# A preLN linear-attention and SwiGLU block, forward and backward: up gradients written over the g2 w2^T buffer, its products two chunks ahead, two norms in other rows, early transposes copied in two parts

## The chip, the cores and the metric

The kernel runs on one core of one Trainium2 chip. The metric is the device time of one execution in microseconds (us). The median of three runs before the change is 838.91 us (838.71 to 839.56); the profiled execution has a span of 838.5 us, and its times count from the start of that span.

The five engines that the text names: PE (TensorE, matmuls and transposes), ACT (ScalarE), DVE (VectorE), POOL (GpSimd) and SyncE (SP in the profile, which here only issues DMAs). Each works through its own row of instructions in the order in which the kernel was written. An instruction that waits holds up everything behind it on its engine.

## The reference

One transformer block in bf16, with 2048 tokens, width 640, 32 heads of 20 and an MLP of width 1728. The output of the block and the gradients of its six inputs are returned.

```python
def _A_ref(x, wqkv, wo):            # linear attention
    q, k, v = split(x @ wqkv)
    phi = lambda t: where(t > 0, t + 1, exp(t)) + 1e-6
    pq, pk = phi(q), phi(k)
    kv = einsum("bhsd,bhse->bhde", pk, v)
    z = einsum("bhsd->bhd", pk)
    o = einsum("bhqd,bhde->bhqe", pq, kv) / (einsum("bhqd,bhd->bhq", pq, z) + 1e-6)
    return o @ wo

def _B_ref(x, w1, w3, w2):          # SwiGLU
    return (silu(x @ w1) * (x @ w3)) @ w2

h = x + _A_ref(layernorm(x), wqkv, wo)
h2 = h + _B_ref(layernorm(h), w1, w3, w2)
out, vjp = jax.vjp(block, x, wqkv, wo, w1, w3, w2)
return out, *vjp(grad_out)
```

In the MLP the backward pass needs, for every token and every one of the 1728 channels f, the product g2 w2^T (g2 is `grad_out`); from it and from gate, up and sigmoid come the gradients of gate and of up.

## The kernel before

The tokens are cut into 16 tiles of 128 rows, and four tiles make a group c = 0 to 3 of 512. The width of 640 is five chunks of 128; the MLP's width is 14 f chunks of 128. The order of the work is written out by hand: the lines of the function are the order on every engine, and buffers (tiles of a pool with a number of `bufs`) come round in turn. A new tile of a name waits until everything that reads or writes the tile that had its buffer is done, DMAs included.

**The front (0 to about 60 us).** For each tile: statistics on DVE (`bn_stats` on each half of the row, `bn_aggr`, variance plus epsilon; lines 144 to 152), the rstd by a power on POOL, the norm on DVE in place (line 155), a transpose into `pqT`, and the k and q products on PE (line 255). Tiles 0 to 7 are transposed on PE into PSUM and copied by ACT (`p1_tr`, line 251); tiles 8 to 15 by DMA. The main loop over tiles (line 460) interleaves tile t's products with the transposes, statistics and norms of later tiles. The loads of x stand in SyncE's row: tiles 0, 1, 2, 3 alone, then 4 and 5, 6 and 7, 8 to 11, 12 to 15 (lines 188 to 424), between transposing loads of w2 and of the first group of `grad_out` (`w2T`, `g2T`).

**The second layer norm.** `f2_at(t)` (line 561) makes the attention output of tile t: ten matmuls with `pqT`, which at that point holds the transposed, scaled q rows of tile t, then the add of x. For tiles 5 to 7 and for the second half of tiles 0 to 3, PE adds x and ACT copies the sum; for the others, DVE adds. Statistics follow. `f2_hn(t)` (line 643) norms the tile into `hn`, which has two buffers of its own, and stores it to HBM for the backward pass; `f2_ht(t)` transposes it (tiles 0 to 3 on PE, later ones by DMA) into `hnT`. Tiles 0 to 3 go through this in the long `run(...)` list (line 777), which mixes in late q tiles, eight early g2 w2^T products (`mlp_ghh`), and loads of `w2T`. Rows named `h2`, of the size of `hn`, have two buffers in the same pool; `r_prod` uses them before this point and the MLP's output rows after it.

**The q rows of later tiles.** For tiles 6 to 15, `r_den(t)` makes the denominators on DVE, and `r_end(t)` scales the rows (line 350) and has SyncE transpose them into `pqT` (line 354, which writes what `f2_at(t)` reads). Their places in the MLP are given by `r_steps` (line 818): in group c = 1, `r_end` of tile 11 comes at the end of f chunk 9.

**The MLP (about 105 to 355 us).** For every group c and f chunk: five matmuls of 512 columns for g2 w2^T (`ghh_chunk`, line 364, copied by ACT into a `ghh` buffer), five for gate, five for up. ACT writes sigmoid(gate), sigmoid(-gate) (`s2`), gate and up; the copies of two chunks make a pair. `ghh` has four buffers of a pair each, `sig`, `s2`, `gate` and `up` two each. The seven DVE products of a pair are put in a list and taken from it during the next pair's chunks (`drain`):

```python
        op(gate, gate, sig)
        op(hh, gate, up, to=hh_d)
        op(s2, gate, s2)
        op(gate, gate, gh, to=gg_d, r0=F)
        op(s2, s2, sig, ALU.add)
        op(s2, s2, up)
        op(up, s2, gh, to=gg_d, q=dmaG)
```

The last one writes the up gradients into `up`, and POOL stores them from there to `gg_d`. Eight chunks of g2 w2^T are made before the MLP starts (`FILL = 8`); in the MLP, chunk n makes product n + `AHEAD`, with `AHEAD = 4`, from chunk 4 of c = 0 on. Between the chunks of group c stand the attention, norm and transpose of the tiles of group c + 1; the function `sides` (line 792) gives the chunk of each. For c = 1, tile 11's `f2_at` comes at the end of chunk 11. From c = 1 on, the output products of the group before (`o2_steps`) are mixed in as well. After the MLP come the gradients of w2, of the second norm, of the attention and of w1 and w3.

Of the kernel before, what the change touches and what calls it, by code (L numbers as in the profile page):

```python
# [9 lines left out]
P = 128  # L10
BF16 = mybir.dt.bfloat16
# [7 lines left out]
S, D, H, F = 2048, 640, 32, 1728  # L19
DH = D // H  # L20
ST, DT = S // P, D // P
FT, FP = 14, 1792
FL = F - 13 * P
W, SC, TPC = 512, 4, 4
# [31 lines left out]
def kernel(  # L56
# [20 lines left out]
    dma, dmaT, dmaG = SY.dma_start, SY.dma_start_transpose, G.dma_start  # L77
# [23 lines left out]
    gg_d = dram.tile([2 * F, S], BF16, name="gg_d")  # L101
    r_v, pk_v, xn_v, hn_v, m_v, pq_v = rows(r_d), rows(pk_d), rows(xn_d), rows(hn_d), rows(m_d), rows(pq_d)

    def pool(name, side="left", space=None):
        kw = dict(space=space) if space is not None else dict(side=side)
        return tc.alloc_tile_pool(name=name, bufs=1, reuse_waits="tile", **kw)
# [6 lines left out]
    x_sb = x_ext[:, :, 0:D]  # L113
# [53 lines left out]
    ln1, ln2 = Stats("ln1"), Stats("ln2")  # L167


    pf = pool("pf", "right")  # L170
# [8 lines left out]
    def load_x(a, b):  # L179
        dma(out=x_sb[:, a:b, :], in_=xS[:, a:b, :])  # L180
# [4 lines left out]
    load_wq(3, 4)  # L185
    load_x(2, 3)
    load_x(3, 4)
    load_x(4, 6)

    mask = cp.tile([P, DT, M_MAX, DH], BF16, name="mask")  # L190

# [24 lines left out]
    def load_g2T(c):  # L216
        g2T[c] = U2.tile([P, DT, W], BF16, name="g2T", tag="g2T", bufs=2)
        dmaT(out=g2T[c][:], in_=goD[c * W:(c + 1) * W, :])
# [16 lines left out]
    def on_act(t):  # L235
        return t > XT_DMA and t % 2 == 0

    def p1_norm(t):
        xn = x_sb[:, t, :]
        (ln1.norm_act if on_act(t) else ln1.norm)(xn, xn, t)  # L240
        if t >= XT_DMA:
            dmaT(out=pqT[:, :, t * P:(t + 1) * P], in_=xn)

    def p1_tr(t, parts=((0, DT),)):
        xn = x_sb[:, t, :]
        for a, b in parts:
            tr = ps.tile([P, DT, P], BF16, name="tr", bufs=2)
            for c in range(a, b):
                T.transpose(tr[:, c, :], xn[:, c * P:(c + 1) * P], ident[:])

            A.copy(out=pqT[:, a:b, t * P:(t + 1) * P], in_=tr[:, a:b, :])  # L251
# [6 lines left out]
    def p1_mm(t, n0):  # L258
        acc = ps.tile([P, 2, 512], F32, name="big", bufs=2)
        for j in range(2):  # L260
            p1_half(acc[:, j, 0:HD], t, n0 + j * HD)
        return acc
# [6 lines left out]
    def phi(acc, dst, then=None):  # L269

        mq, rq = (p1.tile([P, D], BF16, name=n, bufs=b) for n, b in (("mq", 3), ("rq", 3)))
        A.activation(two(mq[:]), acc[:, :, 0:HD], AF.Exp)
        A.activation(two(rq[:]), acc[:, :, 0:HD], AF.Relu)

        def rest():
            V.tensor_scalar(out=mq[:], in0=mq[:], scalar1=1.0, scalar2=1e-6, op0=ALU.min, op1=ALU.add)
            V.tensor_tensor(out=dst, in0=mq[:], in1=rq[:], op=ALU.add)
            if then is not None:
                then()
        held.append(rest)  # L280

    def phi_rest(keep=0):
        while len(held) > keep:
            held.pop(0)()
# [14 lines left out]
    def q_tile(t):  # L299
        q_home(t)  # L300
        phi(p1_mm(t, 0), pqs[t])
# [66 lines left out]
    def ghh_chunk(n, acc):  # L368

        c, fc = divmod(n, FT)  # L370
        mm5_to(acc, w2T, fc, g2T[c])
        if n % 2 == 0:
            ghh[n // 2] = pf.tile([P, 2, W], BF16, name="ghh", bufs=4)
        A.copy(out=ghh[n // 2][:, n % 2, :], in_=acc[:])  # L374
# [5 lines left out]
    def m_part(m, tiles):  # L380
        if m not in macc:
            macc[m] = [ps.tile([P, 512], F32, name="macc", tag=("m", "tr")[m % 2], bufs=2) for _ in range(2)]
        for t in tiles:
            for j, n in enumerate((HD, HD + (m < 3))):
                T.matmul(macc[m][j][:, 0:n], lhsT=pk_all[:, t, m * P:(m + 1) * P],  # L385
                         rhs=x_ext[:, t, j * HD:j * HD + n], start=(t == 0), stop=(t == ST - 1))
# [25 lines left out]
    def load_w2T(a, b):  # L412
        dmaT(out=w2T[:, :, a:b], in_=B_w2[a:b, :])
# [2 lines left out]

    zero_pads()
    load_w2T(0, 2 * P)
    load_x(6, 8)
    load_g2T(0)  # L420
    load_w2T(2 * P, 4 * P)
    load_x(8, 12)
# [8 lines left out]
        ln1.norm(x_sb[:, 0, a:b], x_sb[:, 0, a:b], 0)  # L431
    p1_tr(0, ((0, 2), (2, DT)))
    for t in (1, 2):
        ln1.part(x_sb, t, 1)
        ln1.part(x_sb, t + 1, 0)
        p1_norm(t)
    ln1.part(x_sb, 3, 1)
    trickle += [lambda: load_wq(4, 6)]
    for c0, c1 in ((0, 2), (2, 4), (4, 5)):
# [13 lines left out]
    def group_out(g):  # L453
        sl = slice(g * TPC, (g + 1) * TPC)
        dma(out=pk_v[:, sl, :], in_=pk_all[:, sl, :])
        if g < 2:
            xn_out(g, dma)

    QT = (5, 7, 9, 11)
    for t in range(ST):  # L460
        g, i = divmod(t, TPC)
        k = p1_mm(t, D)
        if t < 3:
            p1_tr(t + 1)
        for n in stat_of.get(t, ()):
            ln1.run(x_sb, n, n + 1)
            if on_act(n):
                ln1.bias(n)
        for n in norm_of.get(t, ()):
            if not on_act(n):  # L470
                p1_norm(n)
        phi_rest(t < 6)
        phi(k, pk_all[:, t, :])
        if 2 <= t < XT_DMA - 2:
            p1_tr(t + 2)
        for n in norm_of.get(t, ()):
            if on_act(n):
                p1_norm(n)
        if t in QT:
            q_tile(QT.index(t))  # L480
        if 2 <= t < 6:
            ghh_chunk(t - 2, ps.tile([P, 2, 512], F32, name="gp", tag="big", bufs=2)[:, 0])
        if t >= 3:
            m_part(0, [t - 3])
        if t >= 11:
            V.memset(bd[:, t - 11, :], 0.0)
            make_mask(t - 11)
        if t >= 9:
            m_part(1, [2 * (t - 9), 2 * (t - 9) + 1])
        if i == 1 and g > 0:  # L490
            group_out(g - 1)
        elif t >= 2 and trickle:
            trickle.pop(0)()
# [65 lines left out]
    hn, hnT, hhT = {}, {}, {}  # L559
# [81 lines left out]
        dma(out=pqs[t], in_=pq_v[:, t, :])  # L641

    def f2_hn(t):
        hn[t] = pf.tile([P, D], BF16, name="hn", bufs=2)
        ln2.norm(hn[t][:], x_sb[:, t, :], t)
        dma(out=hn_v[:, t, :], in_=hn[t][:])

# [22 lines left out]
    def mlp_ghh(n):  # L670
        if n < SC * FT:
            ghh_chunk(n, ps.tile([P, W], F32, name="mm", bufs=4))

    AHEAD = 4

    def mlp(c, fc, between):

        k, i = divmod(fc, 2)
        n = c * FT + fc
        if n >= FILL - AHEAD:  # L680
            mlp_ghh(n + AHEAD)
        gp = mm5(w1, fc, hnT[c])
# [33 lines left out]
    def mlp_pair(c, k, sig, s2, gate, up, gh):  # L716

        hh = hhT[c][:, 2 * k:2 * k + 2, :]

        def op(out, a, b, alu=ALU.mult, to=None, r0=0, q=dma):  # L720
            def go():
                V.tensor_tensor(out=out, in0=a, in1=b, op=alu)
                if to is not None:
                    store(to, r0, c, k, out, q)
            later.append(go)

        sig, s2, gate, up, gh = (x[:] for x in (sig, s2, gate, up, gh))
# [3 lines that stand above are left out]
        op(gate, gate, gh, to=gg_d, r0=F)  # L731
        op(s2, s2, sig, ALU.add)
        op(s2, s2, up)
        op(up, s2, gh, to=gg_d, q=dmaG)

    def o2_steps(c, q=dma, tag="o2"):

# [33 lines left out]
    def run(*steps):  # L771
# [5 lines left out]
    run((q_late, 10, f2_mT), (f2_kv, 2), (f2_kv, 3), (f2_kv, 4), (phi_rest,), (q_late, 11), (f2_wT, 0), (f2_wT, 1),  # L777
        (phi_rest,), (q_late, 12), (f2_wT, 2), (f2_wT, 3), (phi_rest,), (q_late, 13, lambda: f2_wT(4)),
        (r_red, 3), (r_inv, 3), (r_scale, 3), (r_prod, 5), (load_x, 2, 4), (r_T, 3), (q_late, 14), (r_red, 4),
        (r_inv, 4), (r_scale, 4), (r_T, 4), (load_x, 4, 8), (mlp_ghh, 4), (load_w2T, 8 * P, 10 * P), (q_late, 15),  # L780
        (sig_table,), (f2_half, 0, 0), (f2_half, 1, 0), (f2_half, 0, 1), (f2_half, 1, 1), (f2_hn, 0), (mlp_ghh, 5),
        (f2_half, 2, 0), (f2_hn, 1), (f2_m_out,), (load_w2T, 10 * P, 12 * P), (f2_half, 2, 1),
        (f2_ht, 0), (mlp_ghh, 6), (f2_half, 3, 0), (f2_hn, 2), (f2_w_out,), (f2_ht, 1), (f2_half, 3, 1), (phi_rest, 2),
        (q_out, 10, 14), (f2_ht, 2), (f2_hn, 3), (mlp_ghh, 7), (load_w2T, 12 * P, F), (f2_half, 4, 0), (f2_ht, 3),
        (f2_half, 4, 1), (r4_out,), (r_red, 5), (r_inv, 5), (r_scale, 5), (r_out, 5), (r4b_out,), (q_out, 8, 10))
    p1.release()
    pa = pool("pa", "right")
# [4 lines left out]
    def sides(c):  # L792
        side = ({}, {})
        for i in range(TPC):
            k0 = 3 * i - (i == TPC - 1) + (-2, 1, 0)[c]
            for k, pos, f in ((k0 + 2, 1, f2_at), (k0 + 3, 0, f2_hn), (k0 + 3, 1, f2_ht)):
                if c == 0 and f is f2_at:
                    if i == 0:
                        continue
                    f = f2_at0  # L800
                if k0 == -2 and f in (f2_at0, f2_hn, f2_ht):
                    k, pos = (k + 1, 0) if f is f2_at0 else (k + 1, pos)
                if k >= 0:
                    side[pos].setdefault(k, []).append((f, i))
        return side
# [19 lines left out]
    for c in range(SC):  # L825
# [8 lines left out]
        for fc in range(FT):  # L834
# [22 lines left out]
            if c == SC - 1 and fc in (1, 2, 5, 6):  # L857
                i = (1, 2, 5, 6).index(fc)
# [73 lines left out]
    for fc in range(FT - 1):  # L932
        b, i = divmod(fc, 4)
# [347 lines left out]
    for t in range(ST):  # L1281
        c, i = divmod(t, TPC)
# [136 lines left out]
```

## Time and profile before

| | busy us | share of the span |
|---|---|---|
| PE | 820.6 | 98% |
| DVE | 453.7 | 54% |
| ACT | 317.8 | 38% |
| POOL | 103.8 | 12% |

| stretch of the span | PE busy | DVE busy | ACT busy |
|---|---|---|---|
| 0 to 60 us (front) | 53.58 | 43.40 | 39.13 |
| 80 to 100 us (end of the attention) | 19.55 | 16.84 | 16.67 |
| 100 to 160 us (start of the MLP) | 56.29 | 49.19 | 39.94 |
| 160 to 240 us | 77.89 | 72.62 | 45.83 |
| 240 to 340 us | 100.00 | 72.78 | 60.67 |

The busy times are unions of the instructions' spans. Matmuls overlap, and their ends are modelled, so PE's busy time is a little more than the time in which it makes progress. The granted clock of PE is 1.00 in all slices but the last.

Three views are used below. The list of waits tells which engine sat idle at which line, and which instruction or DMA ended the idle time; its numbers are the total, the count and the longest, in us. The timeline lists instructions in order of time, with start and duration; in brackets stands the idle time before it and what ended it. The DMA view tells how long a DMA took from its issue to its landing.

### The profile page before, as it was taken

Reading aid. Unit: us, or ns where it says so; the run is one execution under the profiler, and the core shown is the slowest. Engines: PE = TensorE matmul, PEld = TensorE weight load, DVE = VectorE, ACT = ScalarE, POOL = GpSimd, SP = SyncE. Lnnn points to the kernel's source line nnn. Section 1 sums busy time; section 2 is a strip of 40 time slices with the busy share of each in tenths; the row PEclk is TensorE's granted clock in tenths of the full one; section 3 lists DMA queues with packets and bytes.
Section 4 is the critical chain, followed back from the end, with each engine's and each line's share of the span. In section 5 each row is a group of like instructions: output and inputs, shape, how many; then the busy total and the mean of one; then the engine's idle time right before and its main releaser. Section 6 shows DMA issues by size and latency. Waiting matters only on the chain.

```text
span 838.5 us, 14175 instructions
## 1 busy us (share of the span) xinstructions
PE 820.6 (98%) x5552; PEld 522.9 (62%) x5552; DVE 453.7 (54%) x964; ACT 317.8 (38%) x603; POOL 103.8 (12%) x152
## 2 busy tenths in 40 slices
PE   7999899999999999999999999999999999999998
PEld 5677544455455555677777777777777777555554
DVE  7947798799988666500037777772681545200000
ACT  5855666755555666111122121222211333311111
POOL 2314222112121101000001111110110000000000
PEclk9999999999999999999999999999999999999999
DMA  9996997778575356899967889436998799875661
GB/s 253 295 275 135 215 248 226 238 198 203 132 202 156 110 164 216 212 237 227 277 162 181 186 194 200 98 82 131 204 242 174 155 197 178 213 188 146 163 166 37
DMA packets 324131, 157.59 MB, mean 188 GB/s; under 512 B 235360, under 2 KB 319232, under 8 KB 324064
## 3 DMA queue, kind: packets, MB, share of 16 engines
q1 hardware_dynamic: 294832, 129.04, 65.8%
q10 hardware_dynamic: 24416, 11.23, 6.5%
q0 software_dynamic: 4816, 16.42, 5.8%
q8 instruction: 43, 0.70, 0.4%
q14 instruction: 24, 0.20, 0.1%
HBM read 48.15 MB, written 51.46 MB: 119 GB/s over the span
## 4 chain that ended last, share of the span: by engine, by line
PE 77%; DMA 9%; DVE 8%; issue 2%; SPq 1%; ACT 1%; POOL 0%; DVEq 0%; ACTq 0%; POOLq 0%
PE job L1184 18%; PE mm L364 14%; PE ghn L986 13%; PE gxn L1343 8%; PE gw L939 7%; PE o L746 5%; PE gwo L1071 3%; PE gr L1043 2%; DMA gg_d<-up 2%; PE macc L385 2%; DVE st L147 2%; PE big L255 2%; DMA pqT<-x_sb 2%; PE at L569 1%; DMA small<-m_d 1%
## 5 line engine op out<-in xcount | busy, mean ns | idle before, releaser
L1184 PE MATMUL job<-gb,hnN 128*128 128x432 bf16 x640 | 117.0, 346 | 0.0
L986 PEld LDWEIGHTS <-ggb 128*128 128x128 bf16 x864 | 84.5, 98 | 32.8
L1184 PEld LDWEIGHTS <-hnN 128*128 128x128 bf16 x640 | 62.6, 98 | 54.1
L364 PE MATMUL mm<-pqT,w 128*128 128x512 bf16 x405 | 93.9, 379 | 1.5 <-DMA pqT<-hn 1.1
L364 PEld LDWEIGHTS <-w 128*128 128x128 bf16 x540 | 52.7, 98 | 65.2 <-DMA pqT<-hn 1.6
L1188 ACT CAST obs<-job 128x432 bf16<-128x432 f32 (+1 forms) x60 | 29.1, 485 | 123.8 <-PE job L1184 123.8
L746 PE MATMUL o<-w,hhT 128*128 128x320 bf16 x448 | 67.7, 299 | 0.2 <-DVE h L751 0.2
L364 PE MATMUL mm<-g2T,w2T 128*128 128x512 bf16 x260 | 64.6, 379 | 2.3 <-ACT up L694 2.3
L986 PE MATMUL ghn<-w13a,ggb 128*128 128x320 bf16 x448 | 63.5, 299 | 0.0
L986 PE MATMUL ghn<-w13b,ggb 128*128 128x320 bf16 x416 | 61.4, 299 | 0.0
L746 PEld LDWEIGHTS <-hhT 128*128 128x128 bf16 x448 | 43.8, 98 | 23.9 <-issue 0.4
L939 PE MATMUL gw<-g,hb 128*128 128x320 bf16 x416 | 57.0, 299 | 0.0
L939 PEld LDWEIGHTS <-hb 128*128 128x128 bf16 x416 | 40.6, 98 | 15.7
L374 ACT CAST ghh<-mm 128x512 bf16<-128x512 f32 x52 | 30.7, 590 | 48.5 <-PE mm L364 45.2
L1343 PE MATMUL gxn<-wqT,gT 128*128 128x320 bf16 x320 | 48.7, 299 | 0.0
L1051 POOL TENSOR_TENSOR sz<-Zb,g_h 128x640 f32<-128x640 bf16 x16 | 20.2, 1261 | 200.2 <-DVE g_h L1049 200.2
L364 PEld LDWEIGHTS <-w2T 128*128 128x128 bf16 x280 | 27.2, 98 | 28.1 <-issue 3.3
L255 PE MATMUL big<-wqkv,pqT 128*128 128x320 bf16 x260 | 39.2, 299 | 4.5 <-ACT pqT L251 1.6
L686 ACT ACTIVATE sig<-mm 128x512 bf16<-128x512 f32 x56 | 33.8, 604 | 25.3 <-PE mm L364 22.8
L255 PEld LDWEIGHTS <-pqT 128*128 128x128 bf16 x320 | 30.5, 98 | 18.1 <-DMA pqT<-x_sb 2.3
L998 ACT ACTIVATE gs<-ghn 128x640 bf16<-128x640 f32 x16 | 11.2, 703 | 78.8 <-PE ghn L986 73.9
L1343 PEld LDWEIGHTS <-gT 128*128 128x128 bf16 x320 | 31.2, 98 | 12.4 <-DMA gT<-g_q 0.3
(195 smaller groups left out, 1246.4 us busy)
## 6 DMA issues: line engine op xcount, KB each, us to landing
hh_d<-hhT SPq DMA_DIRECT2D x24, 256.0 KB, 2.6
gg_d<-gate SPq DMA_DIRECT2D x24, 256.0 KB, 3.6
gg_d<-up POOLq DMA_DIRECT2D x24, 256.0 KB, 2.9
ggb<-gg_d SPq DMA_DIRECT2D x6, 896.0 KB, 5.7
ggb<-gg_d SPq DMA_DIRECT2D x6, 832.0 KB, 6.9
out_dram<-obs ACTq DMA_DIRECT2D x40, 108.0 KB, 2.6
ggb<-gg_d SPq DMA_DIRECT2D x2, 1728.0 KB, 12.8
x_sb<-in_A_x_dram SPq DMA_DIRECT2D x5, 640.0 KB, 6.8
```

What stands on the lines that cost most here:

```text
L255: T.matmul(acc, lhsT=pqT[:, c, t * P:(t + 1) * P], rhs=wqkv[:, c, n0:n0 + HD], start=(c == 0), stop=(c == DT - 1))
L364: T.matmul(acc[:], lhsT=w[:, c, fc * P:(fc + 1) * P], rhs=rhs[:, c, :], start=(c == 0), stop=(c == DT - 1))
L374: A.copy(out=ghh[n // 2][:, n % 2, :], in_=acc[:])
L686: A.activation(sig[:, i, :], gp[:], AF.Sigmoid)
L746: T.matmul(o2["ps"][:, 0:HD], lhsT=hhT[c][:, fc, i * P:(i + 1) * P], rhs=w2[:, fc, j * HD:(j + 1) * HD], start=(fc == 0), stop=(fc == FT - 1))
L939: T.matmul(acc[:, j, 0:HD], lhsT=hb[b][:, t, i * P:(i + 1) * P], rhs=g2[:, t, j * HD:(j + 1) * HD], start=(t == 0), stop=(t == ST - 1))
L986: T.matmul(acc[:, j, 0:HD], lhsT=ggb[t // 2][:, k, lo:lo + P], rhs=rhs[:, j * HD:(j + 1) * HD], start=(k == 0), stop=(k == NG - 1))
L1051: G.tensor_tensor(out=heads(sz[t][:]), in0=heads(Zb[:]), in1=per_head(g_hx[:, t, D:]), op=ALU.mult)
L1071: T.matmul(acc[m][:, j, 0:n], lhsT=r_sb[:, t, m * P:(m + 1) * P], rhs=g_hx[:, t, j * HD:j * HD + n], start=(t == 0), stop=(t == ST - 1))
L1184: T.matmul(acc[:, 0:n], lhsT=lhs[:, t, m * P:(m + 1) * P], rhs=rhs(t), start=(t == 0), stop=(t == ST - 1))
L1188: A.copy(out=ob, in_=acc[:, 0:n])
L1343: T.matmul(acc[:, j, 0:HD], lhsT=g, rhs=wqT[:, k, j * HD:(j + 1) * HD], start=(k == 0), stop=(k == 14))
```

## The change

It has six parts, all of them about buffers and order; the arithmetic stays what it was.

- The last DVE product of a pair writes the up gradients over the `ghh` pair rather than over `up`, and the store reads them from there. `up` is then free after its last product, and a `ghh` buffer is held until its store has landed. To allow for that, the g2 w2^T products run two chunks ahead, not four.
- The later part of `w2T` is loaded in two transfers (2 and 3.5 chunks) in place of three, and later.
- `hn` of tiles 2 and 3 is put in the `h2` buffers, so that these norms need not wait for the stores of tiles 0 and 1.
- In the front, DVE norms tile 1 before it takes up the statistics of tile 2, and x tiles 4 to 7 come in one load.
- The PE transposes of tiles 1 to 3 are copied by ACT in two parts (chunks 0 and 1, then 2 to 4), as tile 0's already were, so that the products can start on the first part.
- In `sides`, `f2_at`, `f2_hn` and `f2_ht` of tile 11 come one f chunk earlier in c = 1.

```diff
-    load_x(4, 6)
+    load_x(4, 8)
...
-    load_x(6, 8)
...
     for t in (1, 2):
-        ln1.part(x_sb, t, 1)
-        ln1.part(x_sb, t + 1, 0)
-        p1_norm(t)
+        if t == 1:
+            ln1.part(x_sb, t, 1)
+            p1_norm(t)
+            ln1.run(x_sb, t + 1, t + 2)
+        else:
+            ln1.part(x_sb, t + 1, 0)
+            p1_norm(t)
...
         if t < 3:
-            p1_tr(t + 1)
+            p1_tr(t + 1, ((0, 2), (2, DT)))
...
     def f2_hn(t):
-        hn[t] = pf.tile([P, D], BF16, name="hn", bufs=2)
+        hn[t] = (pf.tile([P, D], BF16, name="hn", tag="h2", bufs=2) if 2 <= t < TPC else
+                 pf.tile([P, D], BF16, name="hn", bufs=2))
...
-    AHEAD = 4
+    AHEAD = 2
...
-        op(up, s2, gh, to=gg_d, q=dmaG)
+        op(gh, s2, gh, to=gg_d, q=dmaG)
...
-        (r_inv, 4), (r_scale, 4), (r_T, 4), (load_x, 4, 8), (mlp_ghh, 4), (load_w2T, 8 * P, 10 * P), (q_late, 15),
+        (r_inv, 4), (r_scale, 4), (r_T, 4), (load_x, 4, 8), (mlp_ghh, 4), (q_late, 15),
...
-        (f2_half, 2, 0), (f2_hn, 1), (f2_m_out,), (load_w2T, 10 * P, 12 * P), (f2_half, 2, 1),
+        (f2_half, 2, 0), (f2_hn, 1), (f2_m_out,), (load_w2T, 8 * P, 10 * P), (f2_half, 2, 1),
...
-        (q_out, 10, 14), (f2_ht, 2), (f2_hn, 3), (mlp_ghh, 7), (load_w2T, 12 * P, F), (f2_half, 4, 0), (f2_ht, 3),
+        (q_out, 10, 14), (f2_ht, 2), (f2_hn, 3), (mlp_ghh, 7), (load_w2T, 10 * P, F), (f2_half, 4, 0), (f2_ht, 3),
...
-            k0 = 3 * i - (i == TPC - 1) + (-2, 1, 0)[c]
+            k0 = 3 * i - (i == TPC - 1) * (1 + (c == 1)) + (-2, 1, 0)[c]
```

## The prediction

> **What bounds the kernel now.** I read the engine totals first, then the waits of TensorE (PE), then the timeline around each wait.
>
> ```profile
> PE 820.6 (98%) x5552; PEld 522.9 (62%) x5552; DVE 453.7 (54%) x964; ACT 317.8 (38%) x603; POOL 103.8 (12%) x152
> ```
>
> PE is busy for 98% of 838.5 us and its clock is full, so no edit of this diff (which leaves PE's matmul count alone) can gain more than the 17.9 us in which PE stands still. Which of it the diff touches is told by PE's own waits (us in total, times, longest):
>
> ```profile
> PE trh L658 <- DVE hn L155: 2.5, 1, 2.5
> PE mm L364 <- ACT up L694: 2.3, 4, 1.0
> PE big L255 <- ACT pqT L251: 1.6, 2, 0.8
> PE mm L364 <- DMA pqT<-hn: 1.1, 1, 1.1
> PE big L255 <- DMA pqT<-x_sb: 1.0, 2, 0.8
> PE tr L249 <- DVE x_sb L155: 0.7, 2, 0.4
> ```
>
> These six rows, 9.2 us, are the targets. Behind the second row, in the waits of 110 to 165 us, and behind the first, in the timeline of VectorE (DVE):
>
> ```profile
> ACT up L694 <- DMA gg_d<-up: 12.7, 6, 3.7
> ```
> ```profile
> 101.55 0.45 DVE L155 TENSOR_SCALAR hn<-x_sb,ln_mv,ln_rs 128x640 bf16<-128x640 bf16 x1 [2.04 <-DMA hn_d<-hn]
> ```
>
> ScalarE (ACT) waits six times for a store to have landed before it may refill an `up` buffer; DVE waits once for a store of `hn` rows. From 240 us to 820 PE is busy 19.5 to 20 of each 20 us, and all that the diff does there is to put two products back (below).
>
> **What the Trainium skill says.** "Perfetto Trace Analysis", Optimization Strategy: a gap that repeats on the engine that should be saturated can mean too few buffers for the next tile. That is the `up` row: two buffers, each held until a store lands. "DMA: Bandwidth & Descriptors", Anatomy of one DMA: a completion carries about 2 us that do not scale with bytes, because the semaphore waits for the last byte's receipt. The trace agrees and is worse under load: `gg_d<-up` takes a median 2.9 us and up to 7.0. So taking a landing out of a short buffer loop is worth more than shrinking the store. "Perfetto Trace Analysis", Optimizing Scalar/DVE Operations: an unsaturated engine that causes bubbles elsewhere may be split into smaller instructions. The trace has both forms: one 640-wide transposed copy is 0.69 us, the two-part one of tile 0 0.82.
>
> **The front (tiles 0 to 7).** DVE does tile 1's norm only after half of tile 2's statistics, and so sat idle 1.91 us until 8.50, when tile 2 had landed (8.48). With the norm ahead, it starts when POOL's `ln_rs` is out, 6.67 + 0.55 = 7.22, inside that idle time; 0.35 us leaves DVE's unbroken row from 8.5 on. PE's transposes of tile 1 (9.40, ready now at 8.96) gain 0.4, and copies in two parts let matmuls start 0.75 us after the transposes (tile 0: 5.52 to 6.27) instead of 1.24 (9.40 to 10.64), three times: 0.4 + 3 x 0.45 = 1.8 us for PE up to tile 3. But DVE runs without a gap from 9.25 to 41.6 and tile 4's transposes already waited for it (0.29 at 15.34), so only its 0.35 survives. Then PE waits at 41.41 for `pqT<-x_sb`, one of a chain of DMAs that land one behind the other from 32 to 58 us. Merging tiles 4 to 7 into one load saves SyncE one issue of 0.57 before the g2 transpose; that and the earlier norms move this chain by something between 0 and 0.6. The merged load lands about 9.76 + 328 KB at 300 GB/s = 10.9, before DVE needs tile 4 at 11.7. I take **-0.3**, ends 0 and -0.9. The extra ACT copies (3 x 0.13) lie in ACT's idle time there (0.70 before each copy).
>
> **`hn` of tiles 2 and 3 in the h2 rows.** hn(2) then no longer waits for the store of hn(0), issued at 97.46 and landed at 101.45. Its rstd was ready at 98.57; DVE reaches it after its statistics at 99.47, so hn(2) moves from 101.55 to 99.47 and the PE transpose from 102.05 to 99.97. The h2 buffers were last read at 90.5 (`rden` reduction). hn(3), 1.9 us behind in the row, is ready at about 101.9, and PE reaches its transpose at 102.0. The whole stage moves by **-2.1**; ends -1.5 and -2.5. The later and larger `w2T` load costs nothing: SyncE has room, and with products two chunks ahead chunk 8 is used two chunks later.
>
> **`up` over the `ghh` buffer, products two ahead (c = 0).** From chunk 4 (115.58) to c = 1 chunk 2 (162.16) PE took 46.6 us. Its content, at 0.216 us a 512-wide matmul: 35 groups of five, 37.8, plus two `at` pairs at 1.63 and 15 output matmuls 2.0: 43.1. So 3.5 us are stalls (the rows show 2.6, since modelled ends overlap). Without the `up` wait two other limits remain. (a) A `ghh` buffer (four) is now held until its store lands, but the fourth pair later wants it two chunks later than `up` was wanted: pair 0's store landed at 122.27, wanted at 121.6, ACT waits 0.7; pair 2's 138.8, wanted 137.4; both inside ACT's idle time. (b) `s2` (`s` in the trace) has two buffers and is free only after its pair's last DVE product: pair 1's at 126.3, while chunk 6 would be there at 122. ACT sits until 126.3, and PE, with four accumulators, stalls about 0.4 at chunk 7. After that, DVE saves its own 2.9 us wait at 139.98 (it waited for ACT, which waited for `up`) and keeps ahead: pair 3's last product 139.4, wanted 139.2; pair 4's 144.7, wanted 145.1. So 3.5 - 0.4 = **-3.1**, ends -1.0 (if DVE's row binds throughout) and -3.5. Two products (2 x 1.08 us PE) leave c = 0 and return in c = 3, where PE is the bound too: zero in sum.
>
> **`at` of tile 11 one chunk earlier (c = 1).** It is meant to end the 1.1 us wait for `pqT<-hn` at 220.92 (in matmul rate 219.61 to 220.92, 1.3). But `at` of tile 11 reads the scaled q rows of tile 11, and what makes them stays where it was:
>
> ```profile
> 202.68 0.82 DVE L350 TENSOR_TENSOR pql<-pql,rden 128x640 bf16<-128x640 bf16 x1
> 203.60 1.21 SPq L354 DMA_TRANSPOSE pqT<-pql  x1
> ```
> ```profile
> pqT<-pql SPq DMA_TRANSPOSE x1, 4.2
> ```
> ```profile
> 198.92 1.52 PE L569 MATMUL at<-Wp,pqT 128*128 128x320 bf16 x10
> 204.47 1.24 PE L364 MATMUL mm<-g2T,w2T 128*128 128x512 bf16 x5
> 208.79 1.52 PE L569 MATMUL at<-Wp,pqT 128*128 128x320 bf16 x10
> ```
>
> The scale on DVE stands after the adds and statistics of tile 10, and these wait for PE's `at` of tile 10 at 198.92. The transpose lands at 203.60 + 4.15 = 207.75. Before, PE came at 208.79, 1.0 us later. Now it comes at 204.47: a **new wait** of 3.3 us, and since the release is counted from PE's own `at` of tile 10, gains further up do not shorten it. Behind it in PE's row stand all later products; DVE's row also stops for it, at tile 11's add, but it has its own slack of 1 us at 208 and 228. hn(11) then lands at about 218, PE needs it at 222.9. Net +3.3 - 1.3 = **+2.0**; ends +2.3, and -1.3 if the transpose came in time. Transposes of this kind took 3.5 to 4.2 us in this stage, so 0.7 is the play.
>
> **Sum.** -0.3 - 2.1 - 3.1 + 2.0 = -3.5: 838.9 becomes **835.4**.
>
> **Rivals.** (1) No new wait: the transpose of tile 11 is there, because DVE runs ahead of PE once c = 0 is freed. Against it: DVE cannot pass the adds of tile 10. -0.3 - 2.1 - 3.1 - 1.3 gives 832.1; chance 0.12. (2) The wait changes its name in c = 0: DVE's row (no idle from 110.35 to 130) holds `s2` and PE gains only 1.0. For it: 46 us of DVE work (110.35 to 162.4 less 5.6 idle) in that stage; against it: DVE's 2.9 + 1.2 + 1.3 us of idle time there are themselves effects of `up`. 838.9 - 0.3 - 2.1 - 1.0 + 2.0 = 837.5; chance 0.15. (3) Slower: the merged load of tiles 4 to 7 lands behind the transposes (12.7, as the load of 6 and 7 did at 11.8) and puts +1.0 on DVE's row, hn brings 1.0, c = 0 nothing, tile 11 costs 2.0: 840.9. Against it: the load is issued ahead of them. Chance 0.06. My forecast has 0.67.
>
> **The numbers.** The range runs from just under rival 1 to just over rival 2, 832.0 to 837.6; some of rival 1, rival 3 and the worst ends stay out. Faster by 0.2% means below 837.2: the forecast less 0.03, rival 1, and nearly half of rival 2: 0.82. Within: 0.12. Slower: 0.06.
>
> **What would show it.** In the profile after: no row ACT `up` on `gg_d`, a small one ACT `ghh` on `gg_d` or on DVE; `trh` on DVE at most 0.5; a new PE row `at` on DMA `pqT<-pql` of about 3 us near 200 us, and none on `pqT<-hn`. Without that new row, near 832; with new rows of `ghh` or `s` that PE waits for, near 837.5; with tile 4's statistics waiting for `x_sb`, the front is wrong.

## The result and the profile after

The changed kernel takes 837.27 us (median of four executions, 835.47 to 837.44) against 838.88 before: a ratio of 0.9974 with a 95% interval of 0.9957 to 0.9992. The medians are 1.6 us apart, the ratio stands for 2.2. Run again beside the experiments, it took 835.94 us (13 executions) against 836.74 (25): 0.9993, interval 0.9981 to 1.0004, which no longer excludes that nothing is gained. It is a small gain, well below the 3.5 us that the prediction summed up. One execution of all those below, of the kernel with the norms alone, took 1448.05 us and is left out of its ratio. The profiled executions had spans of 838.5 and 835.6 us, 2.9 apart, so the first pair of traces flatters the change by about 1.3 us. For this reason a second pair stands beside it below. Its two traces were taken among the experiments, on two chips on which the median of the kernel before is 836.28 us (before) and 836.74 us (changed).

The engine totals of the changed kernel, the line that answers to the one shown of before:

```profile
PE 820.2 (98%) x5552; PEld 522.5 (63%) x5552; DVE 454.3 (54%) x964; ACT 319.5 (38%) x606; POOL 104.4 (13%) x152
```

PE's work is the same; ACT has three copies more, those of the front. PE's own waits in the changed kernel (us in total, times, longest):

```profile
PE at L572 <- DMA pqT<-pql: 4.4, 3, 2.5
PE big L255 <- ACT rq L273: 1.3, 1, 1.3
...
PE tr L249 <- DVE x_sb L155: 1.1, 1, 1.1
...
PE big L255 <- ACT pqT L251: 0.6, 2, 0.3
...
PE trh L662 <- DVE hn L155: 0.4, 1, 0.4
PE big L255 <- DMA pqT<-x_sb: 0.4, 1, 0.4
```

`trh` on DVE has fallen from 2.5 to 0.4, and the rows of `mm` on ACT `up` (2.3) and on `pqT<-hn` (1.1) are gone. In their place the list is headed by a row that was not there: `at` waits three times for the transposed q rows. PE's timeline shows where (start, duration, instruction; in brackets the idle time before it and what ended it):

```profile
98.85 0.45 PE L662 MATMUL trh<-ident,hn 128*128 128x128 bf16 x5 [0.37 <-DVE hn L155]
...
112.84 0.85 PE L572 MATMUL at<-Wp,pqT 128*128 128x320 bf16 x5 [1.57 <-DMA pqT<-pql]
...
130.64 0.85 PE L572 MATMUL at<-Wp,pqT 128*128 128x320 bf16 x5 [0.34 <-DMA pqT<-pql]
...
197.13 1.11 PE L750 MATMUL o<-w,hhT 128*128 128x320 bf16 x7
200.77 1.53 PE L572 MATMUL at<-Wp,pqT 128*128 128x320 bf16 x10 [2.53 <-DMA pqT<-pql]
```

The one at 200.77 is tile 11, which the prediction named. Those at 112.84 (tile 5) and 130.64 it did not. DVE's timeline and SyncE's, with the DMA view of that moment, show the transpose of tile 11 still made by the old schedule. It is issued at 197.14 and lands 3.6 us later, while PE has been done since about 198.2:

```profile
196.29 0.82 DVE L350 TENSOR_TENSOR pql<-pql,rden 128x640 bf16<-128x640 bf16 x1
197.14 1.22 SPq L354 DMA_TRANSPOSE pqT<-pql  x1
```
```profile
pqT<-pql SPq DMA_TRANSPOSE x1, 3.6
```

ACT's waits in the start of the MLP (100 to 165 us) no longer hold a row `up`, which had 12.7 us; these are what took its place:

```profile
ACT s L691 <- DVE ghh L726: 1.9, 2, 1.7
ACT gate L692 <- DMA gg_d<-gate: 1.4, 3, 0.6
...
ACT sig L690 <- DVE s L726: 0.5, 1, 0.5
```

To see what each stage brought, the same PE work was sought in both traces of a pair. The columns give its start before and after, and in brackets the shift, less the 2.16 us of the two products that the change moves from c = 0 to c = 3.

| PE work | first pair | second pair |
|---|---|---|
| products near 45 us (end of the front) | 45.31, 44.24 (-1.06) | 43.32, 43.19 (-0.13) |
| transposes of `hn` of tile 2 | 102.05, 98.85 (-3.20) | 99.67, 97.83 (-1.84) |
| `at` of tile 5 | 114.08, 112.84 (-1.25) | 113.38, 111.43 (-1.95) |
| c = 1, chunk 2 | 162.16, 155.76 (-4.23) | 160.74, 155.74 (-2.83) |
| the product after `at` of tile 11 | 210.15, 206.46 (-1.53) | 208.73, 206.47 (-0.10) |
| c = 2, first gate product | 220.92, 215.92 (-2.83) | 219.69, 215.93 (-1.60) |
| gradients of w2, start | 355.45, 352.25 (-3.20) | 353.87, 352.26 (-1.61) |

The second column reads as a story of giving back: next to nothing kept from the front, 1.8 won at `hn` (3.3 by the next transposes, 103.39 to 100.07), 1.4 lost at tile 5, 0.9 won in c = 0, 2.7 lost at tile 11, 1.5 won at the old wait for `pqT<-hn`. Of the 3.3 about 1.5 is not the change: in the second trace of before, PE runs at half its clock for 3.4 us right behind its wait for `hn` (last section).

### The profile page after: what moved, and what is told of

Read it like the earlier page. It is cut to its first block, busy times and chain, and to the rows that moved or that the text cites. A ratio compares the mean times of both kernels' runs of the same rounds, so it can differ in the third digit from the quotient of the medians.

```text
span 835.6 us, 14195 instructions
## 1 busy us (share of the span) xinstructions
PE 820.2 (98%) x5552; PEld 522.5 (63%) x5552; DVE 454.3 (54%) x964; ACT 319.5 (38%) x606; POOL 104.4 (13%) x152
## 4 chain that ended last, share of the span: by engine, by line
PE 86%; DMA 6%; DVE 5%; SPq 1%; ACT 1%; issue 1%; DVEq 0%; ACTq 0%
PE job L1188 18%; PE mm L364 18%; PE ghn L990 14%; PE gxn L1347 7%; PE o L750 7%; PE gw L943 7%; PE gwo L1075 3%; PE gr L1047 3%; PE macc L385 2%; PE at L572 2%; PE big L255 2%; DMA pkb<-pk_d 1%; DMA small<-m_d 1%; DMA pqT<-pql 1%; PE mm L255 1%; PE dkv L1291 1%
```

## The experiments

Two theories stood against each other for every wait. **A**: a wait that PE shows costs the kernel what it shows. **B**: it only takes the place of a later one, so that taking it away moves the wait on. Every experiment was timed in five rounds beside the kernel before, in three groups, two of them on one chip and the third on another. Each ratio is to the kernel before in the same group.

### The new wait at tile 11

The first experiment is the changed kernel with the old places of tile 11:

```diff
-            k0 = 3 * i - (i == TPC - 1) * (1 + (c == 1)) + (-2, 1, 0)[c]
+            k0 = 3 * i - (i == TPC - 1) + (-2, 1, 0)[c]
```

> The changed kernel with tile 11's attention product, norm and transpose back at their old chunk in c = 1. Theory A (the new wait costs what it shows): the 2.5 us wait of PE at tile 11 goes, a wait for the transposed norm of about 1.3 us comes back at the start of c = 2, net 1.4 us less than the changed kernel, about 835.8 us. Theory B (the wait is slack that VectorE needs, and only moves): as the changed kernel within 0.4 us, about 837.2.

Measured: 832.10 us, ratio 0.9955 (0.9941 to 0.9969), 3.8 us under before. The second keeps the new places and makes the q rows a chunk earlier too:

```diff
-                ... 8: ((r_den, 11),), 9: ((r_end, 11), (r_load, 14)),
+                ... 7: ((r_den, 11),), 8: ((r_end, 11),), 9: ((r_load, 14),),
```

> The changed kernel with the denominators and the scale of q tile 11 one f chunk earlier (chunks 7 and 8 of c = 1 instead of 8 and 9). Theory A: the transpose of tile 11 lands about 4 us sooner, PE no longer waits for it (2.5 us) and the wait at the start of c = 2 stays away: 2.7 us less than the changed kernel, about 834.6. Theory B: VectorE's row is full there, the work brought forward delays tile 10's or another product's operands, and PE waits elsewhere: within 0.5 us of the changed kernel.

Measured: 831.61 us, 0.9949 (0.9935 to 0.9964). The third is the kernel before with nothing but the new places of tile 11:

> The kernel before with one part of the change: attention, norm and transpose of tile 11 one f chunk earlier in c = 1. Theory A (the step of the prediction): a new wait of 3.3 us for the transpose of tile 11's q rows, less the 1.3 of the old wait for its norm: 2.0 us more than before. Theory B (the new wait only takes the place of others, as at tile 5): within 0.5 us of before.

Measured: 840.01 us, 1.0042 (1.0028 to 1.0055), 3.5 us over before. Its list of PE's waits:

```profile
PE at L569 <- DMA pqT<-pql: 3.7, 1, 3.7
```

The three agree on theory A, though the times lie beyond its forecasts: the part costs 3.2 us inside the change (0.9993 against 0.9955, whose intervals do not touch) and 3.5 alone. Alone, the list has no wait for `pqT<-hn` any more, so the wait of 3.7 less that saving of 1.3 would be 2.4. At least part of the rest is a half-clock stretch of 3.4 us that begins just before this wait ends: the ten `at` matmuls take 2.85 us there, not 1.52. What costs is the wait and not the new place, since the place with earlier q rows is as good as the old one. In the trace of the second experiment PE also waits 1.59 us for DVE near 621 us, so another is used here: a version with earlier q rows of tiles 11 and 5 (below) starts `at` of tile 11 at 197.62, the changed kernel of the second pair at 200.77; of these 3.15 us nothing is given back, and the last gradient matmuls begin 3.38 us earlier (713.32 to 709.94).

The 1.3 us that the part was to save had gone without it. The wait for `pqT<-hn` near 220 us is missing also from the list of the first experiment, which has the old places:

```profile
PE at L572 <- DMA pqT<-pql: 1.7, 2, 1.5
PE big L255 <- ACT rq L273: 1.3, 1, 1.3
PE tr L249 <- DVE x_sb L155: 1.1, 1, 1.1
```

There, and with up gradients over `ghh` and `AHEAD = 2` alone (below), the transpose of that norm landed within 2.7 and 2.6 us of its issue, not 4.2 as in the second trace of before. With the norms alone it took 4.3, with the new place of the gradients but `AHEAD = 4` (below) 4.1, and the wait stayed in both. So it is the pair of edits for c = 0, with its two chunks, that ended this wait, by one trace of each kernel. How it shortened the landing was not tested.

### The wait at tile 5

The changed kernel with the q rows of tile 5 made ahead of the products of chunk 7:

```diff
-        ..., (f2_ht, 2), (f2_hn, 3), (mlp_ghh, 7), ...
+        ..., (f2_ht, 2), (f2_hn, 3), (r_red, 5), (r_inv, 5), (r_scale, 5), (r_out, 5), (mlp_ghh, 7), ...
...
-        (f2_half, 4, 1), (r4_out,), (r_red, 5), (r_inv, 5), (r_scale, 5), (r_out, 5), (r4b_out,), (q_out, 8, 10))
+        (f2_half, 4, 1), (r4_out,), (r4b_out,), (q_out, 8, 10))
```

> The changed kernel with the reduction, scale and transpose of q tile 5 right after the norm of tile 3, ahead of tile 4's adds. Theory A: PE's wait of 1.57 us for the transposed q rows of tile 5 at 113 us, which the changed kernel shows, goes, and the time falls by 1.0 to 1.6 us, to about 836. Theory B: this wait only stood ahead of one that VectorE's row gives anyway (s of pair 1 at chunk 6), so PE waits at chunk 6 or 7 instead: under 0.4 us less than the changed kernel.

Measured: 835.99 us, 0.9991 (0.9983 to 1.0000), the same as the changed kernel's 0.9993. The wait at tile 5 is gone, and `at` of tile 5 starts 2.2 us earlier than in the first trace of the changed kernel (112.84 to 110.60). At `at` of tile 7 (130.64 to 130.16) 0.5 is left, and by that much this trace had been ahead before c = 0 began (transposes of `hn` of tile 3 at 100.60, not 101.10). That speaks for theory B; the intervals of the two ratios alone would leave room for about 1 us. Its two remaining waits for q rows are that of tile 11 and that of tile 7 at 130 us, which is 1.5 us here, against 0.3 and 0.8 in the two traces of the changed kernel:

```profile
PE at L572 <- DMA pqT<-pql: 4.1, 2, 2.6
```

Tiles 11 and 5 together, and then tile 7 as well (its `r_den` and `r_end` from chunks 4 and 5 to chunks 3 and 4 of c = 0):

> The changed kernel with the q rows of tile 11 scaled and transposed one f chunk earlier, and those of tile 5 earlier too. Theory A: each wait of PE for a transpose of q rows costs what it shows, so 3.2 us (tile 11) plus up to 1.7 (tile 5) less than the changed kernel. Theory B for tile 5 alone (the next wait takes it over, as its single run showed): 3.2 to 3.6 less. If both only move: under 1 us less.

Measured: 831.86 us, 0.9940 (0.9927 to 0.9952): the gain of tile 11, with nothing for tile 5 that the intervals could tell from none.

> The changed kernel with the q rows of tiles 11, 7 and 5 scaled and transposed earlier. Theory A (a wait of PE for the transpose of q rows costs what it shows): the last such wait of c = 0, 1.3 us near 130 us, goes, and the time is 1.3 us below that of the version with tiles 11 and 5 alone (ratio to before 0.9940 there, 0.9925 here). Theory B (in c = 0 the waits only move, to ACT's s2 and gate buffers): within 0.3 us of it, with PE waiting for ACT or for other transposes instead.

Measured: 832.16 us, 0.9949 (0.9934 to 0.9963). No wait for q rows is left, and nothing is won. In PE's list its place is taken by ACT:

```profile
PE mm L364 <- ACT gate L692: 2.1, 2, 1.1
```

So in c = 0 these waits only show a bound that lies elsewhere. The next section looks for it.

### The parts that were to win

The kernel before once more, for a second trace:

> The kernel before once more, for its trace beside those of the experiments. Two single parts that leave the front alone began c = 0 with the first 45 us already 1.7 and 2.3 us shorter than in the first trace of before. Theory A (that stretch differs from execution to execution, through the chain of transfers of x): this trace too has the last first-stage products near 43.3 us, not 45.3, and the kernels that were compared with the first trace gained that much less. Theory B (the first trace is typical): 45 us again, and the two single parts shorten the front in a way the diff does not tell. The time is that of before under both.

Measured: 836.14 us, 1.0000 (0.9989 to 1.0011); the products near 45 us start at 43.32. Theory A: the first trace of before had a late front, with 1.1 us of waits of PE for loads of `wqkv` that the second has not, and of the 1.06 us that the first pair shows there, 0.13 is left.

The changed kernel with the old front (both loads, the old order of tiles 1 and 2, copies in one part):

> The changed kernel with the four front edits undone (loads of x tiles 4 to 7, VectorE's order at tiles 1 and 2, copies in two parts). Theory A (front worth what the two traces show): 1.0 us slower than the changed kernel, about 838.2. Theory B (the forecast: swallowed by the chain of DMAs that land one behind the other): 0 to 0.6 us slower, about 837.5.

Measured: 837.01 us, 1.0006 (0.9995 to 1.0017), against 0.9993 for the changed kernel; the intervals overlap. Its work on PE is 0.9 to 1.8 us later than that of the changed kernel (second pair) up to 13 us, 0.1 later at 27.4 and 0.5 from 40 us; about 0.6 of the early difference is two waits for loads of `wqkv` that the trace of the changed kernel lacks. PE's timeline in the changed kernel of the second pair shows what takes the early gain away:

```profile
10.96 1.64 PE L255 MATMUL big<-wqkv,pqT 128*128 128x320 bf16 x10 [0.30 <-ACT pqT L251]
12.62 0.45 PE L249 MATMUL tr<-ident,x_sb 128*128 128x128 bf16 x5
14.20 0.45 PE L249 MATMUL tr<-ident,x_sb 128*128 128x128 bf16 x5 [1.13 <-DVE x_sb L155]
```

The wait for the copy in front of tile 2's products is 0.30 (0.78 in the second trace of before), and the gain is spent at 14.20: PE waits 1.13 us for DVE's norm of tile 4, where before it waited 0.29.

The norms of tiles 2 and 3 alone, in the kernel before:

> The kernel before with one part of the change: the norms of tiles 2 and 3 in the h2 rows. Theory A (the 2.1 us that DVE waited for a store moves the whole rest): 2.1 us less than before. Theory B (in c = 0 ACT still waits for the stores of up gradients, which swallows a part of it): 0 to 1 us less, with ACT's waits for gg_d above the 12.7 us of before.

Measured: 834.63 us, 0.9979 (0.9969 to 0.9988), 1.8 us less. Against the second trace of before the transposes of `hn` of tile 2 are 1.5 us earlier and those of tile 3 3.0. Of the 3.0 about 1.5 is the half-clock stretch in the trace of before. At c = 1, chunk 2, the shift is 3.2 us (160.74 to 157.53), so c = 0 swallowed none of it, although ACT waits for `gg_d` as it did in the first trace. At the end 2.4 are left. That speaks for theory A, but not for all of its size: among executions with a mean clock of 0.999 or more, the norms bring 1.0 us (834.7 in 10 against 835.8 in 13). The rest of the 1.8 goes with half-clock stretches, which 12 of 25 executions of before had and 1 of 11 of this kernel.

The up gradients over `ghh`, with products two chunks ahead, alone in the kernel before:

> The kernel before with one part of the change: up gradients over the ghh pair, products two chunks ahead. Theory A (the six waits of ACT for a landed store made the stall of PE in c = 0): 3.0 us less than before, plus up to 1.3 if the wait for the transposed norm of tile 11 goes without being touched: 3.0 to 4.3 less. Theory B (DVE's row holds the s2 buffers and PE gains little): 1.0 less. The row ACT up on gg_d is gone under both.

Measured: 834.12 us, 0.9969 (0.9957 to 0.9981), 2.6 us less. The time is near theory A, but the trace puts it elsewhere. Less the moved products, the shift against the second trace of before is 1.0 us at c = 1, chunk 2 (160.74 to 157.56), as theory B has it. It is 2.5 at the start of c = 2 (219.69 to 215.02), where the wait for `pqT<-hn` is missing.

The same with `AHEAD` left at 4:

> The kernel before with the up gradients over the ghh pair, but products still four chunks ahead. Theory A (with products four ahead a ghh buffer is wanted two chunks sooner than its store has landed): a new row ACT ghh on gg_d of 8 us or more in c = 0, and less than 1 us of the 2.6 that the pair of edits brought. Theory B (four ghh buffers are enough at either distance): 2.6 us less than before, as with two chunks ahead.

Measured: 844.56 us, 1.0108 (1.0090 to 1.0126), 8 to 9 us slower. Theory A named the row but not its size. ACT's waits from 100 to 165 us and PE's over the whole span:

```profile
ACT ghh L374 <- DMA gg_d<-ghh: 15.2, 4, 6.1
```
```profile
PE mm L364 <- ACT ghh L374: 6.1, 3, 2.9
```

Held until its store has landed, a `ghh` pair four chunks ahead is wanted before it is free. Both waits stop ACT's row, but this one is the longer: 15.2 us, where ACT in the two traces of before waited 12.7 and 4.8 for stores of `up`, and PE waits 6.1 for ACT's copies, where it waited 2.3 and 2.0. Two half-clock stretches are in this trace as well. Going down to two chunks is not a detail of the edit but what makes it work.

### What bounds c = 0 after the change

The chain of waits in the changed kernel of the second pair, from 100 to 165 us, followed back from its end (start, duration, what; some pieces left out; the row of DVE ahead of it runs with hardly a gap from 106.3 to 121.4):

```profile
123.63 0.73 DVE pql L350
124.36 0.32 DVE s L726
124.69 4.91 DMA pqT<-pql
...
129.64 0.85 PE at L572 x5
...
131.31 2.17 PE mm L364 x10
...
134.09 5.27 DMA gg_d<-gate
...
139.43 0.16 ACT gate L692
139.59 6.93 DMA gg_d<-gate
...
146.60 0.59 ACT gate L692
...
147.24 3.40 PE mm L364 x15
```

First DVE's row, then the landing of tile 7's q transpose, then twice the landing of a store of gate gradients. `gate` has two buffers and is held until its store lands, as `up` was before the change. ACT's waits say the same:

```profile
ACT gate L692 <- DMA gg_d<-gate: 4.2, 3, 2.0
ACT s L691 <- DVE ghh L726: 2.7, 2, 2.1
```

The first two links are common to all traces that have the edits of c = 0 with `AHEAD = 2` and the old place of tile 7's q rows (landings of 4.6 to 4.9 us). The gate stores are not: they stand in the chain twice in this trace and once in those of the first two experiments, and not in the first trace after the change nor in those with an earlier tile 5.

Counted from the transposes of `hn` of tile 3, `at` of tile 7 starts after 29.3 to 29.6 us, whether `at` of tile 5 had to wait or not, and c = 1, chunk 2, comes after 54.5 to 55.0 us in six of the seven traces of the changed kernel and its variants; the one above takes 55.7. So tile 5 is worth nothing because tile 7's q rows come off DVE's row no earlier. With tile 7's rows made earlier its `at` starts after 28.6 us, and a wait of 1.0 us at 140.67 for ACT's gate copy, with the landing of a gate store (5.4 us) ahead of it, gives most of that back (54.9). That more `gate` buffers would free it was not tried.

## Why the prediction was right, and where its steps were not

The time fell into the stated range, at its upper end: 837.27, where the forecast was 835.4 and rival 2 said 837.5. This was in part luck. The 0.6 us of the later measurement, taken from the 838.9 of the forecast, would have been 838.3, outside the range. Two terms of the sum were wrong, c = 0 and tile 11, and both made the gain too large.

- **Front, -0.3**: right in kind. 0.13 in the second pair, and DVE's row takes the gain as argued (it has one gap, of 0.26 us at 10.83, where the prediction saw none); the experiment cannot tell 0.3 from nothing or from 1. The merged load was in time: what PE waits for at 14.20 is DVE's norm, and DVE's statistics from 7.77 to 14.12 run without a wait for `x_sb`.
- **`hn` in the h2 rows, -2.1**: right. 2.1 in the first pair (3.20 less 1.06 of the front), 1.7 in the second, and 1.8 us (1.0 to 2.6 by the interval) as a single edit. That the end keeps so much is owed in part to fewer half-clock stretches, of which the prediction had none. The later load of `w2T` shows no wait in PE's list.
- **c = 0, -3.1**: the term that failed. From `at` of tile 5 to chunk 2 of c = 1 the first pair gives 3.0, but 1.75 of this had just been lost at tile 5; counted from the transposes of tile 3 it is 1.2, and in the second pair nothing is won (0.9 behind tile 5, 1.4 lost at it). The single edit, which has no wait at tile 5, brings 1.0. That is the lower end of the term, and DVE's row is what binds, as rival 2 had it, though what PE then waits for is the q rows of tile 7. The `ghh` and `s2` loops behaved as worked out: no wait of ACT for `gg_d<-ghh` in the first trace after and 0.3 us in the second, 1.9 and 2.7 us for `s`. What the step left out is the transpose of q rows at the end of DVE's row, and behind it the `gate` loop, the same kind of loop with the same two buffers. Its stall of 3.5 us was PE's in one trace, and was taken to be wholly that of `up`.
- **A gain without a step**: the same pair of edits also ended the wait for `pqT<-hn` near 220 us, 1.3 to 1.5 us. This is why the single edit brings 2.6 us and not 1.0.
- **Tile 11, +2.0**: the mechanism was right and the size was off. The new wait was forecast at 3.3 us; PE's list has 2.5, and the products behind it move by 2.7 in both pairs. The landing of 3.6 us in place of 4.2 accounts for most of the difference. But inside the change the credit of 1.3 was already the other edit's, so the part costs 2.7 us at its place and 3.2 us by the ratios, not 2.0. Rival 1 (no new wait, 832.1) is refuted for this kernel. Where the wait is taken away the time is 832.10 and 831.61, but beside a kernel before of 836.7, not 838.9.
- **Tile 5**: not foreseen. The argument for tile 11, that q rows stay where they were while PE comes earlier, holds for every tile whose `at` comes earlier, and the prediction asked it of tile 11 alone. It cost 1.4 to 1.75 us at its place. As tile 7's rows bind behind it, the experiments cannot tell its cost in the end from nothing.

In the experiments the single edits bring 1.8 and 2.6 us, the change without tile 11's new place 3.8 (2.6 to 4.9), and tile 11 takes back 3.2. What is left is 0.6. The prediction's 3.5 was too high by the c = 0 term and by the credit at tile 11. Its ceiling of 17.9 us is not strict, since PE's busy time runs over its progress, but nothing here came near it. The interval of the first measurement, 0.7 to 3.6 us, just admits it.

The Trainium skill's "DMA: Bandwidth & Descriptors", Anatomy of one DMA, which the prediction cited for about 2 us in each completion, describes DMAs from POOL's queue, such as the store of `up`. The landings that now decide here are of DMAs that SyncE issues, and they took longer: 3.6 to 4.9 us for a q transpose of 160 KB and 5.3 to 6.9 for a gate store of 256 KB. Every short buffer loop with a landing in it deserved a price, not only the one with the longest row.

## What to carry to other kernels

When a consumer is moved earlier, list all that it reads and find where each is made; a producer left at its old place turns the move into a wait, here 3.2 us of a gain of 3.8. When one buffer loop with a store in it is opened, price the other loops of the same stage before crediting the whole stall, and note how far ahead the lender's own producer runs: the same borrowed buffer lost 8 us at four chunks ahead and won 2.6 at two. A wait worth removing is one whose shift is still there several stages later in the aligned traces. And a new wait can cost more than it shows, as the last section tells.

## What was not expected of the hardware

The same kernel varies more than the effects studied here. The kernel before took between 834.3 and 839.6 us in the 71 executions beside the experiments, and its front ended at 45.31 us in one trace and 43.32 in another, with the same instructions. A single pair of traces gave 1.06 us for the front and 3.0 for c = 0 where a second pair gave 0.13 and 0.9.

One cause shows in the traces: a wait of PE can cost more than its length. Twelve waits of PE of 2.1 us or more stand in the traces of this case. At seven of them, in five traces, the granted clock falls to 0.50 for 3.41 us, beginning between 0.7 us before and 1.3 us after the wait's end; away from such waits it falls only at the end of the span. The second trace of before, and the same products in the changed kernel of the second pair:

```profile
99.67 0.62 PE L658 MATMUL trh<-ident,hn 128*128 128x128 bf16 x5 [2.12 <-DVE hn L155]
100.08 2.34 PE L364 MATMUL mm<-g2T,w2T 128*128 128x512 bf16 x5
```
```profile
97.83 0.45 PE L662 MATMUL trh<-ident,hn 128*128 128x128 bf16 x5 [0.37 <-DVE hn L155]
98.12 1.24 PE L364 MATMUL mm<-g2T,w2T 128*128 128x512 bf16 x5
```

One such stretch costs up to 1.7 us of PE's work and lowers the mean clock of an execution by 0.002. Of the 71 executions of before, 30 have a mean clock of 0.998 or less; they take 837.6 us on average, the others 835.8. Of the 13 of the changed kernel it is 8. Of 33 executions of the five kernels whose traces show no such wait, it is 2. The wait alone does not decide it: five of the twelve, among them those of 2.50 us at `hn` in the first trace of before and of 2.53 at tile 11 in the first after, were not followed by one. What does was not tested.

Steps of this size need a second trace of both kernels, and a ratio over many executions.

The landing of one and the same transpose of a norm (tile 11, issued near 215 us in the second trace of before) took 4.2 us there, 2.7 and 2.6 in two variants, and 4.1 and 4.3 in two others, with 1.3 to 1.5 us of PE's time depending on it.
